# Loading the weights' 64-row remainders first, on two queues, and alternating two V products in the first step

## The chip, the cores and the metric

The kernel runs on one core of a Trainium2 chip. The metric is the device time of one execution in microseconds. TensorE (PE) does the matrix products, VectorE (DVE) and ScalarE (ACT) the elementwise work and the copies out of PSUM, GpSimd (POOL) some fills and a power, and SyncE (SP) issues most transfers. ACT and POOL can issue transfers too, each on a queue of its own.

## The reference

Two layers of the same kind run one after the other over 2048 rows of width 576. Each layer adds a memory-augmented attention, and then a gated feed-forward block:

```
for s in range(n_seg):                      # 64 segments of 32 rows
    h = concat([mem, x[s]])                 # 8 memory rows + 32 rows, width 576
    q, k, v = h @ Wq, h @ Wk, h @ Wv        # 32 heads of 128
    p = softmax(where(mask, q @ k.T * scale, -1e9))
    o = (p @ v) @ Wo
    mem = o[:8]; out[s] = o[8:]
x = x + attention(layernorm(x));  x = x + (silu(n @ w1) * (n @ w3)) @ w2   # n = layernorm(x)
```

The memory makes the 64 segments of a layer a chain: a segment's first products need the memory rows that the segment before it gave.

## The kernel before

The kernel works in steps. Step t does segment t of the first layer and, eight steps later, the segment of the second layer that has become ready, so there are 72 steps and the first eight hold one layer only. The width of 576 is four blocks of 128 rows and a remainder of 64 rows; every product with Wq, Wk and Wv has a part for the four blocks and a part for the remainder.

The weights stay in SBUF. Tile W (128 x 9 x 4096) holds the four blocks of Wq in places 0 to 3 and those of Wk in places 4 to 7; place 8 holds the remainder of Wq in partitions 0 to 63 and that of Wk in partitions 64 to 127. Tile WV holds the four blocks of Wv and then its remainder, the even groups of 512 columns in partitions 0 to 63 and the odd ones in 64 to 127. Wo goes to WO in four groups of eight heads. All of it is loaded once, at the start, on SP's queue, in this order: load_qk for the first half of the heads (eight pieces of 512 KB, then two remainder pieces of 256 KB), load_qk for the second half, load_v (four blocks of 1 MB, then two remainder pieces of 256 KB), load_o (four groups). ACT's queue brings the first 128 rows of x (tile XN) and the first memory (load_m0).

A step's products are these. QK units 0 to 7 (four heads each) make q and k, in qk (32 matmuls in step 0) and qk_tail (8). A score (SC), a softmax, a transposition of the probabilities (TR), the product of probabilities and V (PV) and the product with Wo (WO and its tail) follow for each of four groups of heads. V is made in v_mm, for two sets of rows: vx for the rows of x (VX) and vm for the strip with the memory rows (VM). In step 0 each has 32 main matmuls, four blocks of Wv by two banks by four column strips, and 8 for the remainder. Each of the two sets fills two PSUM banks, and eight evictions of 512 columns by ACT or DVE (v_ev) bring them into tile V.

Everything is laid down by a planner (plan). make_nodes writes the program as nodes with an engine, a modelled duration, what they depend on, a priority and the buffers that they take and free. The planner then simulates: for each engine it takes the node that could start first, and among several the one with the lowest priority number. A node of engine "AD" goes to ACT or to DVE, whichever can take it. The modelled order on each engine is kept in the program. PE alone isn't chosen in this way: its order is written out by hand as a string of letters (FIRST for the beginning), a letter for each node: Q and q for a QK unit's blocks and remainder, S for scores, T for TR, P for PV, O and o for WO, X and x for VX's main part and remainder, V and v for those of VM. In v_nodes the evictions depend on both parts; those of VX have priority -0.77 in step 0, those of VM 0.14.

Records of engine instructions stand on the lines of the helpers: L578 matmuls, L581 ACT, L584 DVE, L587 transfers on SP's queue, L590 on ACT's, L593 on POOL's.

Of the kernel before, what the change touches and what calls it, by code (L numbers as in the profile page):

```python
# [9 lines left out]
ACT = mybir.ActivationFunctionType  # L10
# [3 lines left out]
P = 128  # L14
R64 = 64
D = 576
# [10 lines left out]
NG = 4  # L27
# [157 lines left out]
def ewh(*ns):  # L185
# [2 lines left out]


FIRST = (  # L190
    "maQqqqQQSQqqqQTQSqqQSQSXxvVPTPTOPOTOoooPOoQQQqqVSqqvQQqqSQQqqSQTXPSxTOPTPOTOPoooOoaQQqqqqQSvQVSqQQqTQSqqQSPTPOOT"
    "ooPTPOOooQQqqqvqSVQQQqSTQqqQPSqQOSoTXPTOPTOPxooOoQQpQqqqqQSVSnvqQFffqFQQTSqqPQOToSfFPWTOPfFTOPFOfoooWQQfqqqQSvVF"
    "qfQFQWSqqQFSfQTQPqqfFOTSoWPFTOPfxXTFPOOoooWQQqqfqQQSfqFSvVfqqQFQWSqTQQPFqffTOSoPWOTFPFTOPfaOoooWQFQqqfQSVvqqfFQQ"
    "SqWQQqqqQSTPSTbOPoXTOPTxxPOOoooXqqQpQQqqSVvnQFFSfqQqfqQQTSqfFPQTOPSofWTOPFOTFPWOoooFQqqffQQqSQQQqqgqGTSWPQQfqqFF"
# [21 lines left out]
class Opt:  # L216

    qk, qkt, sc, tr, pv, wo, wog, vm = 0.0079, -0.0342, 0.0268, 0.1447, 0.0406, 0.2653, 0.0725, 0.1407
    vmt, vx, vxt, ff, fft, win, w2, gstep = -0.0231, 0.2313, 0.0843, 0.2124, -0.1839, 0.8 * (LAG - 4), 0.1943, 0.0624
    ustep, mode_pen, hor, wait, bulk, ff_split, last_win, tail_at = 0.0315, 0.1194, 0.0162, 0.141, 0.02, False, 2.5, -1.5  # L220


def make_nodes(em, nseg, pools, o=Opt, dma_bw=230e3, load_bw=400e3):
# [4 lines left out]
    def node(*a, **k):  # L228
        n = Node(*a, **k)
        nodes.append(n)  # L230
        return n

    def banks(n=2):
        return [Slot("bank") for _ in range(n)]

    nst = nseg + LAG
    kb = lambda rows, cols: rows * cols * 2
# [9 lines left out]
    def load(name, nbytes, prio, fn, deps=()):  # L247
        return node("DMA", nbytes / load_bw, fn, deps=deps, prio=prio, name=name, lat=2.0)

    ld_m0 = node("ACT", 0.1, em.load_m0(), prio=-90, name="m0", lat=2.5)  # L250
    ld_h = [load("ldqk", kb(512 + 2 * R64, 4096), half - 9.0, em.load_qk(half)) for half in (0, 1)]
    ld_v = [load("ldv", kb(512 + 2 * R64, 4096), -7.0, em.load_v())]
    ld_o = [load("ldo", kb(1024, 576), g - 6.0, em.load_o(g)) for g in range(NG)]

    b = banks(1)
# [303 lines left out]
class Emitter:  # L559
# [79 lines left out]
    def load_qk(self, half):  # L639
        def f(n):  # L640
            h = slice(half * 2048, (half + 1) * 2048)
            for kind, wd in ((0, self.a.wq), (1, self.a.wk)):
                for c in range(4):
                    self.dma(self.T.W[:, 4 * kind + c, h], wd[c * P:(c + 1) * P, h])
            for kind, wd in ((0, self.a.wq), (1, self.a.wk)):
                self.dma(self.T.W[kind * R64:(kind + 1) * R64, 8, h], wd[4 * P:D, h])
        return f

    def wv(self, tail):
# [4 lines left out]
    def load_v(self):  # L654
        def f(n):
            for c in range(4):
                self.dma(self.wv(False)[:, c, :], self.a.wv[c * P:(c + 1) * P, :])
            for r in (0, 1):
                self.dma(self.wv(True)[r * R64:(r + 1) * R64, :].rearrange("p (q n) -> p q n", q=NG),
                         self.a.wv[4 * P:D, :].rearrange("p (q r n) -> r p q n", q=NG, r=2)[r])  # L660
        return f

    def load_o(self, g):
# [131 lines left out]
        return lambda n: self.cp(n, self.T.XTB[:, :, bi * P:(bi + 1) * P], self.lnps(b))  # L795


    def v_mm(self, t, b, strips, tail):

        HTt = self.ht(t)  # L800
        W = self.wv(tail)
        first = self.begin(b)
        for c in ((4,) if tail else range(4)):
            for r in (0, 1):
                for p0, c0, q, m, row in strips:
                    out = self.bk(b[r])[p0:p0 + m, :]
                    if tail:
                        rr = slice(r * R64, (r + 1) * R64)
                        self.mm(out, HTt[rr, 4, c0:c0 + m], W[rr, q * 512:(q + 1) * 512], first, True, tile_position=(r * R64, p0))
                    else:  # L810
                        w0 = (2 * q + r) * 512
                        self.mm(out, HTt[:, c, c0:c0 + m], W[:, c, w0:w0 + 512], first and c == 0, c == 3, tile_position=(0, p0))

    def vg(self, t, g, b, tail):

# [33 lines left out]
        return [(p0, m, row, 2 * q + r) for p0, _, q, m, row in strips]  # L849

    def vx(self, t, k, b, tail):
        return lambda n: self.v_mm(t, b, self.vx_strips(t, k), tail)

    def vm(self, t, k, b, tail):
        return lambda n: self.v_mm(t, b, self.vm_strips(t, k), tail)

    def v_ev(self, b, p0, width, row, blk):
        return lambda n: self.cp(n, self.T.V[row:row + width, blk, :], self.bk(b)[p0:p0 + width, :])
# [317 lines left out]
def kernel(  # L1176
# [26 lines left out]
    em = Emitter(nc, tc, T, a, nseg)  # L1203
    pools = dict(POOLS)
    nodes = make_nodes(em, nseg, pools)

    wp = ctx.enter_context(tc.tile_pool(name="wts", bufs=1))
# [94 lines left out]
```

## Time and profile before

| | us |
|---|---|
| median of 4 runs | 2703.91 |
| lowest and highest | 2702.74, 2704.65 |
| the profiled execution, its own time | 2701.56 |
| its span in the profile | 2699.8 |
| PE busy | 2628.1 (97%) |
| DVE busy | 2090.4 (77%) |
| ACT busy | 1367.3 (51%) |
| mean granted PE clock | 0.993 |

The profile is one execution. Its time lies 1.76 us above its span, and 2.35 us below the median of the four runs. Times of instructions are counted from the start of the span. Brackets behind an instruction give the engine's idle time before it and what ended it. "PEclk" is the granted share of PE's clock. The DMA share is the mean busy share of 16 DMA engines.

### The profile page before, as it was taken

The numbers are of one execution on the slowest core, as the hardware profiler recorded it, in microseconds if no ns is written. First come the engines' busy times: TensorE is split into PE (matmuls) and PEld (weight loads), VectorE is DVE, ScalarE is ACT, GpSimd is POOL, SyncE is SP. The second block draws the span as 40 slices with busy tenths as digits, with TensorE's granted clock in tenths as the row PEclk, the third lists the DMA queues.
The fourth block names the chain that finished last, engine by engine and source line by source line (L and its number), as shares of the span: only waits on it lengthen the run. The fifth ranks groups of instructions, "written<-read, shape, count | busy, mean of one in ns | idle before, by whom it ended". The sixth has DMA issues, their size and how long they took to land.

```text
span 2699.8 us, 126553 instructions
## 1 busy us (share of the span) xinstructions
PE 2628.1 (97%) x55714; PEld 2225.9 (82%) x55795; DVE 2090.4 (77%) x5376; ACT 1367.3 (51%) x4025; POOL 333.6 (12%) x400
## 2 busy tenths in 40 slices
PE   5999999999999999999999999999999999999998
PEld 3788888888888888888888888888888888888886
DVE  4777887877778777777877777787787777787876
ACT  2655554545545454554545455464544546454553
POOL 1111110110101011010101101010110101011110
PEclk8999999999999999999999999999999999999999
DMA  9064524234342423434243343433334342434358
GB/s 316 4 186 123 159 84 118 80 110 126 99 134 80 121 86 110 125 102 131 79 119 88 110 125 96 129 87 115 92 110 125 96 129 70 128 95 141 114 157 262
DMA packets 483225, 321.42 MB, mean 119 GB/s; under 512 B 26376, under 2 KB 477328, under 8 KB 482160
## 3 DMA queue, kind: packets, MB, share of 16 engines
q1 hardware_dynamic: 479488, 306.22, 38.5%
q8 instruction: 437, 7.16, 1.1%
q0 software_dynamic: 3024, 6.93, 0.9%
q14 instruction: 116, 0.95, 0.1%
q10 hardware_dynamic: 160, 0.16, 0.0%
HBM read 308.49 MB, written 2.36 MB: 115 GB/s over the span
## 4 chain that ended last, share of the span: by engine, by line
PE 87%; ACT 4%; DVE 3%; DMA 3%; issue 1%; SPq 1%; POOL 0%; DVEq 0%; ACTq 0%; POOLq 0%
PE bank L578 87%; ACT V L581 3%; DMA W<-in_B_w_dram 2%; DVE SME L584 1%; DMA W<-in_A_Wk_dram 1%; DVE STAT L584 1%; DMA WV<-in_A_Wv_dram 1%; DVE V L584 1%; SPq L587 1%; ACT SME L581 0%; ACT XTB L581 0%; ACT PTS L581 0%; ACT QKT L581 0%; DVE PB L584 0%; DVE OT L584 0%
## 5 line engine op out<-in xcount | busy, mean ns | idle before, releaser
L578 PEld LDWEIGHTS <-W 128*128 128x128 bf16 (+1 forms) x29520 | 1237.8, 98 | 148.2 <-issue 43.6
L578 PE MATMUL bank<-HT,W 128*128 128x80 bf16 (+3 forms) x23040 | 811.2, 196 | 22.7 <-DMA W<-in_A_Wq_dram 10.3
L578 PE MATMUL bank<-XTB,W 128*128 128x256 bf16 (+3 forms) x6480 | 661.0, 261 | 7.1 <-DMA W<-in_B_w_dram 6.1
L581 ACT ACTIVATE QKT<-bank 128x256 bf16<-128x256 f32 (+3 forms) x1587 | 365.9, 316 | 368.8 <-PE bank L578 349.9
L981 POOL MEMSET PB<- 128x1024 bf16 x288 | 274.2, 952 | 1815.9 <-PE bank L578 1303.4
L578 PE MATMUL bank<-OT,WO 128*128 128x80 bf16 (+3 forms) x11520 | 406.0, 198 | 0.6 <-DVE OT L584 0.3
L581 ACT ACTIVATE V<-bank 64x512 bf16<-64x512 f32 (+1 forms) x616 | 346.5, 584 | 109.4 <-PE bank L578 104.2
L578 PEld LDWEIGHTS <-WO 128*128 128x128 bf16 (+1 forms) x11520 | 378.7, 102 | 15.6 <-issue 5.6
L578 PE MATMUL bank<-WV,HT 128*32 128x512 bf16 (+5 forms) x3160 | 357.1, 385 | 14.8 <-issue 8.8
L578 PE MATMUL bank<-W2C,HTT 128*128 128x288 bf16 x2240 | 315.1, 286 | 0.0
L584 DVE TENSOR_TENSOR PB<-SME,STAT 40x128 bf16<-40x128 f32 (+4 forms) x912 | 275.3, 336 | 14.9
L584 DVE TENSOR_REDUCE STAT<-SME 104x8 f32<-104x320 f32 (+1 forms) x576 | 273.9, 476 | 13.6 <-ACT SME L581 8.3
L581 ACT ACTIVATE HTT<-bank 128x512 bf16<-128x512 f32 (+1 forms) x324 | 179.6, 555 | 181.9 <-PE bank L578 179.9
L578 PEld LDWEIGHTS <-HT 128*32 128x32 bf16 (+4 forms) x3240 | 137.1, 97 | 158.0 <-issue 39.7
L584 DVE SCALAR_TENSOR_TENSOR XR<-bank,XR 128x288 f32<-128x288 f32 x576 | 246.8, 450 | 16.6 <-PE bank L578 8.5
L578 PEld LDWEIGHTS <-HTT 128*128 128x128 bf16 x2304 | 210.4, 98 | 48.7 <-issue 0.2
L581 ACT ACTIVATE OT<-bank 128x320 bf16<-128x320 f32 (+1 forms) x398 | 149.3, 405 | 167.1 <-PE bank L578 165.9
L584 DVE CAST QKT<-bank 128x192 bf16<-128x192 f32 (+2 forms) x461 | 125.0, 317 | 136.2 <-PE bank L578 134.8
L584 DVE SCALAR_TENSOR_TENSOR HTT<-HTT,bank 128x512 bf16<-128x512 bf16 (+1 forms) x324 | 202.5, 625 | 33.8 <-ACT HTT L581 30.0
L584 DVE TENSOR_TENSOR HTT<-HTT,bank 128x512 bf16<-128x512 bf16 (+1 forms) x324 | 203.7, 629 | 30.6 <-DVE HTT L584 0.5
L581 ACT ACTIVATE PTS<-bank 128x320 bf16<-128x320 f32 (+1 forms) x385 | 144.4, 401 | 162.7 <-PE bank L578 123.6
L581 ACT ACTIVATE SME<-SME 104x320 f32<-104x320 f32 (+1 forms) x288 | 135.5, 470 | 139.7 <-DVE SME L584 136.9
(61 smaller groups left out, 1804.9 us busy)
## 6 DMA issues: line engine op xcount, KB each, us to landing
W<-in_B_w_dram SPq DMA_DIRECT2D x612, 256.0 KB, 3.5
W2C<-in_B_w_dram SPq DMA_DIRECT2D x306, 288.0 KB, 3.2
W<-in_B_w_dram SPq DMA_DIRECT2D x612, 32.0 KB, 3.3
W<-in_B_w_dram SPq DMA_DIRECT2D x16, 512.0 KB, 8.7
WO<-in_A_Wo_dram SPq DMA_DIRECT2D x4, 1152.0 KB, 16.3
XR<-in_A_x_dram POOLq DMA_DIRECT2D x16, 288.0 KB, 2.8
WV<-in_B_w_dram SPq DMA_DIRECT2D x8, 576.0 KB, 7.3
W<-in_A_Wq_dram SPq DMA_DIRECT2D x8, 512.0 KB, 8.9
```

The source lines that it names most:

```text
L578: self.ch("PE", self.nc.tensor.matmul(out, lhsT=lhsT, rhs=rhs, start=start, stop=stop, skip_group_check=True, **k))
L581: self.ch("ACT", self.nc.scalar.activation(*a, **k))
L584: self.ch("DVE", getattr(self.nc.vector, fn_)(*a, **k))
L587: self.ch("SP", self.nc.sync.dma_start(out=out, in_=in_))
L981: return lambda n: self.ch("POOL", self.nc.gpsimd.memset(self.T.PB[:, pb.i], 0.0))
```

## The change

Three things change.

The remainders are no longer loaded with their halves. A new load_tails brings them first: SP's queue gets the whole remainder of Wq (64 rows of 4096 columns, partitions 0 to 63) and the lower half of Wv's; ACT's queue gets the whole remainder of Wk (partitions 64 to 127) ahead of x, and the upper half of Wv's behind the first memory.

In step 0 vx no longer emits its main matmuls. It keeps its banks and rows, and vm emits them together with its own: for each block of Wv first those of VX, then those of VM.

In FIRST the letters "XxvV" of step 0 become "XVxv".

```
 FIRST = (
-    "maQqqqQQSQqqqQTQSqqQSQSXxvVPTPTOPOTOoooPOo...
+    "maQqqqQQSQqqqQTQSqqQSQSXVxvPTPTOPOTOoooPOo...
...
-    ld_h = [load("ldqk", kb(512 + 2 * R64, 4096), half - 9.0, em.load_qk(half)) for half in (0, 1)]
-    ld_v = [load("ldv", kb(512 + 2 * R64, 4096), -7.0, em.load_v())]
+    ld_t = [load("ldt", kb(3 * R64, 4096), -10.0, em.load_tails(0)), node("ACT", 0.1, em.load_tails(1), prio=-120, name="ldt", lat=6.0)]
+    node("ACT", 0.1, em.load_tails(2), prio=-80, name="ldt", lat=6.0)
+    ld_h = [load("ldqk", kb(512, 4096), half - 9.0, em.load_qk(half)) for half in (0, 1)]
+    ld_v = [load("ldv", kb(512, 4096), -7.0, em.load_v())]
...
-            for kind, wd in ((0, self.a.wq), (1, self.a.wk)):
-                self.dma(self.T.W[kind * R64:(kind + 1) * R64, 8, h], wd[4 * P:D, h])
+    def load_tails(self, what):
+        def f(n):
+            if what < 2:
+                d, wd = (self.dma, self.a.wq) if what == 0 else (self.adma, self.a.wk)
+                d(self.T.W[what * R64:(what + 1) * R64, 8, :], wd[4 * P:D, :])
+            if what != 1:
+                r = what // 2
+                (self.adma if r else self.dma)(self.wv(True)[r * R64:(r + 1) * R64, :].rearrange("p (q n) -> p q n", q=NG),
+                                               self.a.wv[4 * P:D, :].rearrange("p (q r n) -> r p q n", q=NG, r=2)[r])
+        return f
...
-            for r in (0, 1):
-                self.dma(self.wv(True)[r * R64:(r + 1) * R64, :].rearrange("p (q n) -> p q n", q=NG),
-                         self.a.wv[4 * P:D, :].rearrange("p (q r n) -> r p q n", q=NG, r=2)[r])
...
-    def v_mm(self, t, b, strips, tail):
+    def v_mm(self, t, sets, tail):
...
-        first = self.begin(b)
+        sets = [(b, strips, self.begin(b)) for b, strips in sets]
         for c in ((4,) if tail else range(4)):
-            for r in (0, 1):
-                for p0, c0, q, m, row in strips:
+            for b, strips, first in sets:
+                for r in (0, 1):
+                    for p0, c0, q, m, row in strips:
...
     def vx(self, t, k, b, tail):
-        return lambda n: self.v_mm(t, b, self.vx_strips(t, k), tail)
+        def f(n):
+            if t == 0 and not tail:
+                self.x0 = (b, self.vx_strips(t, k))
+                return
+            self.v_mm(t, [(b, self.vx_strips(t, k))], tail)
+        return f
...
-        return lambda n: self.v_mm(t, b, self.vm_strips(t, k), tail)
+        return lambda n: self.v_mm(t, ([self.x0] if t == 0 and not tail else []) + [(b, self.vm_strips(t, k))], tail)
```

More of the change, by code (lines that the diff above doesn't have):

```diff
@@ L190 @@
 FIRST = (
-    "maQqqqQQSQqqqQTQSqqQSQSXxvVPTPTOPOTOoooPOoQQQqqVSqqvQQqqSQQqqSQTXPSxTOPTPOTOPoooOoaQQqqqqQSvQVSqQQqTQSqqQSPTPOOT"
+    "maQqqqQQSQqqqQTQSqqQSQSXVxvPTPTOPOTOoooPOoQQQqqVSqqvQQqqSQQqqSQTXPSxTOPTPOTOPoooOoaQQqqqqQSvQVSqQQqTQSqqQSPTPOOT"
     "ooPTPOOooQQqqqvqSVQQQqSTQqqQPSqQOSoTXPTOPTOPxooOoQQpQqqqqQSVSnvqQFffqFQQTSqqPQOToSfFPWTOPfFTOPFOfoooWQQfqqqQSvVF"
@@ L795, in xtb_write @@
         return lambda n: self.cp(n, self.T.XTB[:, :, bi * P:(bi + 1) * P], self.lnps(b))
-    def v_mm(self, t, b, strips, tail):
+    def v_mm(self, t, sets, tail):
         HTt = self.ht(t)
         W = self.wv(tail)
-        first = self.begin(b)
+        sets = [(b, strips, self.begin(b)) for b, strips in sets]
         for c in ((4,) if tail else range(4)):
-            for r in (0, 1):
-                for p0, c0, q, m, row in strips:
[L806 to L812, printed above, removed]
+            for b, strips, first in sets:
+                for r in (0, 1):
+                    for p0, c0, q, m, row in strips:
+                        out = self.bk(b[r])[p0:p0 + m, :]
+                        if tail:
+                            rr = slice(r * R64, (r + 1) * R64)
+                            self.mm(out, HTt[rr, 4, c0:c0 + m], W[rr, q * 512:(q + 1) * 512], first, True, tile_position=(r * R64, p0))
+                        else:
+                            w0 = (2 * q + r) * 512
+                            self.mm(out, HTt[:, c, c0:c0 + m], W[:, c, w0:w0 + 512], first and c == 0, c == 3, tile_position=(0, p0))
     def vg(self, t, g, b, tail):
```

## The prediction

> **What bounds the kernel now.** I read the shares of busy time first: PE is busy 97% of a span of 2699.8 us, and only the first of the 40 slices shows it half idle. The change touches nothing but the first load of the weights and the V products of step 0, so the question is how much earlier step 0 can end, since all later work hangs on it. The windows view of that stretch (columns: length, then busy us and count of PE, PEld, DVE, ACT, POOL, then PEclk, DMA share, GB/s):
>
> ```profile
> 14.00:17.00 3.00, 2.58 (x39) 1.39 (x37) 0.00 (x0) 0.00 (x0) 0.00 (x0) 1.00 1.03 229
> 18.00:26.00 8.00, 3.16 (x117) 2.95 (x112) 3.53 (x10) 1.71 (x6) 0.00 (x0) 0.94 1.03 408
> 27.00:30.00 3.00, 0.00 (x0) 0.00 (x0) 0.00 (x0) 0.00 (x0) 0.00 (x0) 0.50 1.06 238
> 32.00:39.00 7.00, 5.89 (x184) 5.49 (x184) 4.10 (x12) 1.65 (x6) 0.95 (x1) 0.77 1.01 419
> 40.00:46.00 6.00, 2.32 (x36) 0.81 (x29) 2.87 (x9) 0.68 (x2) 0.00 (x0) 0.96 1.08 222
> 46.00:55.00 9.00, 6.83 (x100) 3.29 (x99) 6.59 (x12) 5.99 (x14) 1.44 (x2) 0.50 1.08 389
> ```
>
> The DMA engines are busy throughout, yet move half as much in three stretches. Those are just the stretches of the 64-row remainders: of Wq and Wk for the first half of the heads, for the second half, and of Wv. Now PE's timeline, for what waits on them:
>
> ```profile
> 31.46 0.21 PE L578 MATMUL bank<-HT,W 64*128 64x40 bf16 x1 [10.30 <-DMA W<-in_A_Wq_dram]
> 32.36 1.63 PE L578 MATMUL bank<-HT,W 64*128 64x40 bf16 x47 [0.68 <-DMA W<-in_A_Wk_dram]
> ...
> 39.75 1.48 PE L578 MATMUL bank<-WV,HT 128*32 128x512 bf16 x24
> 43.94 0.62 PE L578 MATMUL bank<-WV,HT 128*32 128x512 bf16 x8 [2.71 <-DMA WV<-in_A_Wv_dram]
> 45.27 0.47 PE L578 MATMUL bank<-WV,HT 64*32 64x512 bf16 x4 [0.72 <-DMA WV<-in_A_Wv_dram]
> 46.36 4.58 PE L578 MATMUL bank<-WV,HT 64*32 64x512 bf16 x44 [0.61 <-DMA WV<-in_A_Wv_dram]
> 51.20 0.31 PE L578 MATMUL bank<-PTS,V 128*128 128x40 bf16 x4 [0.26 <-ACT V L581]
> ...
> 59.53 1.19 PE L578 MATMUL bank<-OT,WO 128*128 128x40 bf16 x40 [0.27 <-ACT OT L581]
> ```
>
> The reader is to see: x's V product does three blocks of Wv (24 matmuls), waits 2.71 us for the fourth, then for each half of the remainder. Only then do the strip's 32 main matmuls begin, inside the 44. PE's clock is 0.50 by then, and the first P.V product comes at 51.20, released by an eviction of V. ACT's timeline shows those evictions, four of x and four of the strip:
>
> ```profile
> 45.79 2.39 ACT L581 ACTIVATE V<-bank 32x512 bf16<-32x512 f32 x4 [3.02 <-PE bank L578]
> 50.56 2.51 ACT L581 ACTIVATE V<-bank 32x512 bf16<-32x512 f32 x4 [2.38 <-PE bank L578]
> ```
>
> [...] 4 KB packets take about 159 ns when 128 rows are written, about 286 ns in the remainders. [...] at 4 to 5 us x (ACT's queue) and Wq (SP's) move together at 389 GB/s. Two half-partition transfers at once appear nowhere in this trace. [...] here the clock is 0.50 from 25 to 35 and from 45.5 to 59 us[...].
>
> **The load, step by step.** Sizes are from the DMA issues: four 256 KB pieces of Wq and Wk remainders (1.05 MB), two of Wv (0.52 MB), 1.57 MB in all. Removed ahead of Wv's last block are two pairs of 0.52 MB at 229 and 238 GB/s: 2.3 + 2.2 = 4.5 us. Added at the front are all six (now four issues of 512, 512, 256 and 256 KB). At the full 408 GB/s they take 3.85 us; at 229, 6.9 us. The price of pairing is unknown: the 16 engines could all be on the lower half together and then on the upper, which would gain nothing. I take 370 GB/s, near the top[...]: 4.25 us. So the mains of the first half come 4.25 us later, those of the second half 2 us later than now, Wv's blocks 0.25 us earlier.
>
> The semaphore events of the trace give each transfer's 16 shares: Wv's fourth block arrives from 39.81 to 43.90. Its late shares fall into the slow stretch of the remainders behind it; a Wo piece, with nothing slow behind it, spreads over 2.3 us (46.78 to 49.09). New arrival of the whole block: 39.81 - 0.25 + 2.3 = **41.9** instead of 43.9; 41.5 with perfect pairing, 44.5 with none.
>
> **What comes late at the front, and its cover.** Wk's remainder goes ahead of x and mem0 on ACT's queue; the fourth issue follows them. ACT itself first computes at 11.58, so some 0.5 us per issue cost nothing. SP's queue gets two issues more at its head and six fewer later. x landed 5.47; with 1.05 MB ahead it lands at 8 to 10. The layer norm on DVE waited for DVE's own memsets until 8.36 anyway, so HT is written up to 1.7 us later than 13.84, while the first QK needs Wk's fourth block, now at 15.5 + 4.25 = 19.7. Cover 4 us. POOL issues nothing of this.
>
> QK units 0 to 3 (15.97 to 21.16 now) end at about 25.1, and the remainder products of units 3 to 5 follow at once: 24 matmuls, some 0.7 us. Then PE waits for the second half's mains, at about 30.5 instead of 32.35 for its last remainder. The 7.4 us from there to the V products shrink by 15 remainder matmuls (0.4 us): V starts at about 37.5. Its 48 matmuls for three blocks, at 1.48/24 = 0.062 each, end at 40.5, inside the wait for 41.9. Alternation so puts 24 strip matmuls where PE idled; were the clock half, they'd end at about 43.4 and cost 1.5 us of the gain.
>
> **From Wv's last block to P.V.** Left are 16 main matmuls, at 0.060 each (32 in 1.91 us in the next step, full clock): 0.96 us; then x's remainder, 8 in 0.41, whose first half frees the first bank after 0.2: the first eviction starts 1.2 us after the block. The strip's remainder lies beside it. But x and strip now finish together, so no matmuls of the strip hide x's evictions: eight of x must pass ACT and DVE (0.588 and 0.686 each) before the strip's first, by the priorities. Five on ACT are 3.0 us. So P.V comes 4.2 us after the block, 46.1, where it took 7.3. **Gain 5.1 us.** The 3.1 us less than now are: 24 strip matmuls and two remainder waits gone, partly paid back by naked evictions. Half clock would cost 0.96 + 0.2 more, gain 3.9.
>
> From there to the end of the step ACT, DVE and PE have the same work in the same order as from 51.20 on, at the same half clock[...]. I let the shift pass unchanged. One bound: Wo's last group. The view by tile says:
>
> ```profile
> L587 SPq DMA_DIRECT2D WO<-in_A_Wo_dram x4: 385/4479/7723, 31.4 to 46.2; - x4
> ...
> DMA to landing us min/median/max: 12.5/16.3/19.8
> ```
>
> The last is issued at 46.2 and lands 12.5 later, 58.7, for products at 59.53. Its stretch gets back 2.0 us (the W remainders at full rate) and 2.6 (1.33 MB in 40 to 46 us, against 3.4 us at 389 GB/s): 54.1. Shifted by 5.1 the products start at 54.4. So it just holds, and caps the gain near 5.4 to 6.
>
> **Sum.** Against the profiled execution: 2701.56 - 5.1 = 2696.5 (span 2699.8 to 2694.7). That execution lies 2.35 under the median of four, 2703.91, so against the median: 2698.8; I say 2698.9. About 0.2%, 5.4 us, is what a measurement can tell from no change, so the forecast lies just inside it.
>
> **Rivals.**
> Pairing does nothing (the change doesn't do what it says): the remainders take 6.9 us at 229 GB/s, the block lands at 44.5, P.V at 48.7, gain 2.5: 2701.4. [...]
>
> The load gains more: engines stay closer together, so shares spread over 1 us and not 2.3, Wo's last group comes as much earlier, and the clock stays full through the O products (groups of 32 in 0.96 instead of 1.23 us, some 1.5 us in all). Gain 6 to 8: 2696.9. For it: the early Wq blocks spread over 0.8 us only. Against: Wv's first, unslowed by remainders, already spread over 2.2.
>
> Slower: the orders of ACT and DVE for the whole program come from a planner's modelled times; only PE's order is written out. The new nodes shift those times. If later evictions thereby fall behind another on their engine, each 0.30 us QKT eviction so delayed in all of the 72 steps costs 21.6 us: 2703.9 - 5 + 21.6 = 2720.5. It decides from 0.15 us per step (5 + 5.4 over 72). For it: ACT and DVE share evictions by the model. Against: past step 0 PE sets the model's times as well, so a pure shift leaves the choices as they were.
>
> **How the numbers follow.** The forecast, 0.72, with its own range of 3.6 to 6.2 us gain (half clock to perfect pairing and shorter spread): 0.30 of it beyond 5.4 us, 0.42 within. Pairing void 0.10, within. More gain 0.10, faster. Slower 0.08. Sums: 0.40 faster, 0.52 the same, 0.08 slower. Range 2696.0 to 2703.0: it holds the forecast, the void pairing and most of the larger gain, and leaves out the planner's case and the ends.
>
> **What would show it.** Right: over 350 GB/s from 2 to 7 us and no dip at 14, 27 and 40; V's matmuls in runs of 16; Wv's last block at about 42; P.V at about 46; Wo's last group near 54. Wrong: a first 1.5 MB at 230 GB/s, a clock of 0.5 through the V products, evictions of the strip ahead of x's, or a distance from P.V to the end that isn't what it was.

## The result, and the profile after

| | before | after |
|---|---|---|
| median of all runs, us | 2702.74 (62 runs) | 2698.44 (43 runs) |
| ratio to before, 95% interval | | 0.9985, 0.9981 to 0.9989 |
| span of the profiled execution, us | 2699.8 | 2695.9 |

The ratio makes the gain 4.1 us (0.0015 of 2702.7), with an interval from 3.0 to 5.1 us. That is less than 0.2%, as forecast; the forecast gain was 5.0 us. The forecast had the gain's size. It did not have the way to it.

First the windows view of the kernel after, over the stretches that were shown of the kernel before; the columns are the same, and the last number is GB/s:

```profile
14.00:17.00 3.00, 0.00 (x0) 0.00 (x0) 0.00 (x0) 1.21 (x5) 0.00 (x0) 1.00 1.02 406
18.00:26.00 8.00, 7.92 (x173) 5.26 (x173) 1.73 (x5) 0.91 (x3) 0.00 (x0) 1.00 1.03 410
27.00:30.00 3.00, 0.19 (x1) 0.10 (x1) 1.23 (x4) 0.20 (x1) 0.00 (x0) 1.00 1.02 407
32.00:39.00 7.00, 5.36 (x148) 5.01 (x149) 4.22 (x12) 1.47 (x5) 0.95 (x1) 0.59 1.02 420
40.00:46.00 6.00, 4.45 (x87) 1.98 (x86) 4.66 (x12) 2.46 (x5) 0.00 (x0) 1.00 1.06 382
```

The three slow stretches at 14, 27 and 40 us are gone. They have moved to the front, as these windows of the same profile show:

```profile
2.50:6.50 4.00, 0.00 (x0) 0.00 (x0) 3.67 (x6) 0.00 (x0) 3.34 (x10) 1.00 1.02 233
9.00:13.00 4.00, 1.00 (x10) 0.76 (x11) 2.38 (x10) 0.03 (x1) 0.56 (x1) 1.00 1.04 335
```

233 GB/s is the half rate of the kernel before (229 and 238). The DMA packets of the trace say how: the 64 packets of 8 KB of SP's queue (Wq's remainder) begin between 2.10 and 4.02 us, the 64 of ACT's queue (Wk's) between 3.97 and 6.40. There were two queues and both issues began at 0.75 us, and the halves were still written one after the other.

PE's timeline of the kernel after, through step 0 (matmuls are now recorded on line L580):

```profile
31.40 0.21 PE L580 MATMUL bank<-HT,W 128*128 128x40 bf16 x1 [1.09 <-DMA W<-in_A_Wk_dram]
32.67 1.01 PE L580 MATMUL bank<-HT,W 128*128 128x40 bf16 x25 [1.06 <-DMA W<-in_A_Wk_dram]
...
40.28 4.19 PE L580 MATMUL bank<-WV,HT 128*32 128x512 bf16 x80
47.35 0.27 PE L580 MATMUL bank<-PTS,V 128*128 128x40 bf16 x4 [2.88 <-ACT V L583]
...
55.52 1.19 PE L580 MATMUL bank<-OT,WO 128*128 128x40 bf16 x40 [0.29 <-ACT OT L583]
```

The second half of Wk releases PE at 32.67, where its remainder did at 32.36: the load has gained nothing there. The V products start half a microsecond later than before. But then all 80 run in one piece, with no wait for Wv, and the P.V products come 3.85 us earlier than 51.20. Ahead of them stands the bare wait for V's evictions, 2.88 us. They make one run on ACT:

```profile
44.30 4.79 ACT L583 ACTIVATE V<-bank 32x512 bf16<-32x512 f32 x8 [1.00 <-PE bank L580]
```

The last WO products start 4.0 us earlier than 59.53, and the span is 3.9 us shorter: in this pair of profiles what step 0 gained reached the end. That the two agree so well is chance. The same kernel profiled again (e11) started the last WO products at 58.04, only 1.5 us earlier than before, and its span was 2.6 us shorter (2697.2). From the start of the second step to the end, the fourteen profiles of this document took between 2636.1 and 2644.5 us.

### The profile page after: what moved, and what is told of

Same layout as the page of the kernel before. It is cut to its first block, busy times and chain, and to the rows that moved or that the text cites. A ratio compares the mean times of both kernels' runs of the same rounds, so it can differ in the third digit from the quotient of the medians.

```text
span 2695.9 us, 126547 instructions
## 1 busy us (share of the span) xinstructions
PE 2624.4 (97%) x55714; PEld 2224.5 (83%) x55795; DVE 2089.9 (78%) x5376; ACT 1366.6 (51%) x4025; POOL 333.2 (12%) x400
## 4 chain that ended last, share of the span: by engine, by line
PE 87%; ACT 4%; DVE 3%; DMA 3%; issue 1%; SPq 0%; POOL 0%; ACTq 0%; DVEq 0%; POOLq 0%
PE bank L580 87%; ACT V L583 3%; DMA W<-in_B_w_dram 2%; DVE SME L586 1%; DMA W<-in_A_Wk_dram 1%; DVE STAT L586 1%; DVE V L586 1%; SPq L589 0%; ACT SME L583 0%; DMA WV<-in_A_Wv_dram 0%; ACT XTB L583 0%; ACT QKT L583 0%; ACT PTS L583 0%; DVE PB L586 0%; DVE OT L586 0%
## 5 line engine op out<-in xcount | busy, mean ns | idle before, releaser
L580 PEld LDWEIGHTS <-W 128*128 128x128 bf16 (+1 forms) x29520 | 1238.0, 98 | 143.2 <-issue 44.8
L580 PE MATMUL bank<-HT,W 128*128 128x80 bf16 (+3 forms) x23040 | 812.1, 197 | 18.2 <-ACT HT L583 6.3
L580 PE MATMUL bank<-XTB,W 128*128 128x256 bf16 (+3 forms) x6480 | 660.9, 261 | 6.2 <-DMA W<-in_B_w_dram 5.1
L580 PE MATMUL bank<-OT,WO 128*128 128x80 bf16 (+3 forms) x11520 | 406.1, 198 | 0.8 <-DVE OT L586 0.5
L580 PEld LDWEIGHTS <-WO 128*128 128x128 bf16 (+1 forms) x11520 | 378.8, 102 | 15.8 <-issue 5.8
L580 PE MATMUL bank<-WV,HT 128*32 128x512 bf16 (+5 forms) x3160 | 353.6, 381 | 12.0 <-issue 10.0
L580 PE MATMUL bank<-W2C,HTT 128*128 128x288 bf16 x2240 | 315.2, 286 | 0.0
L580 PEld LDWEIGHTS <-HT 128*32 128x32 bf16 (+4 forms) x3240 | 136.5, 96 | 152.8 <-issue 33.2
L580 PEld LDWEIGHTS <-HTT 128*128 128x128 bf16 x2304 | 209.7, 98 | 48.6 <-issue 0.4
```

The source lines that it names most:

```text
L580: self.ch("PE", self.nc.tensor.matmul(out, lhsT=lhsT, rhs=rhs, start=start, stop=stop, skip_group_check=True, **k))
```

## Experiments

All ratios are to the kernel before, with the 95% interval. Where two kernels are compared, each was run beside the kernel before on the same chip; medians of different groups of runs aren't compared, since the kernel before's own median lies between 2700.72 and 2702.74 us from group to group. Theory A, formed on the traces: the second queue does nothing, the remainders cost at the front what they cost elsewhere, and the gain is that nothing slow stands behind a block that PE waits for. Theory B: two queues save load time. Theory C, the prediction's: the alternation brings most of the gain.

### Each part alone

e1_load_only has the new load and the old V order; e10_load_only_again is the same kernel once more; e11_changed_again is the changed kernel beside it.

```
-    "maQqqqQQSQqqqQTQSqqQSQSXVxvVPTP...
+    "maQqqqQQSQqqqQTQSqqQSQSXxvVPTP...
-            if t == 0 and not tail:
+            if False:
-        return lambda n: self.v_mm(t, ([self.x0] if t == 0 and not tail else []) + [(b, ...
+        return lambda n: self.v_mm(t, [(b, self.vm_strips(t, k))], tail)
```

> The new order of the load alone; step 0's V products in the old order (x's four blocks, x's remainder, the strip's remainder, the strip's four blocks). Theory A (the new load order alone brings the gain: nothing slow stands behind Wv's last block any more, so all of Wv is there by 42.6 us, and the alternation only trades hidden evictions against hidden products): x's products end near 43.6 us, their eight evictions run beside the strip's 32 products at full clock (2 us), P.V starts at 46.5 to 47.0 instead of 47.35, ratio to the kernel before 0.998 to 0.9985, gain 4 to 5 us. Rival C (the alternation brings the gain, as the prediction had it: 3.1 of its 5.1 us): P.V at 49 to 50.5 us, gain under 2 us.

> The new order of the load alone, a second time, beside the changed kernel on the same chip. If the alternation is worth nothing once the load is in the new order: within 1 us of the changed kernel's median. If the alternation is worth the 24 products that it takes out of the end of the V products, at half clock 2.5 us, less the evictions it lays bare: the changed kernel 1 to 2 us faster than this.

> The changed kernel itself, beside the new load order alone. Ratio to the kernel before 0.998 to 0.999 as on record; its difference to the load order alone is the alternation's worth: 0 if the alternation is worth nothing once the load is in the new order, 1 to 2 us otherwise.

e2_alternate_only keeps load_qk, load_v and make_nodes' load lines of the kernel before, and takes the rest of the change.

> The alternating V products of step 0 alone; the old order of the load. Theory A: Wv's last block comes at 43.9 us and its remainder's two halves at 45.3 and 46.3 as in the kernel before, so evictions can't start before about 46.2 us; five on ACT later P.V starts at 49.3 to 49.8 us instead of 51.2, gain 1.5 to 2 us. Rival C: P.V at 47 to 48 us, gain 3 to 4 us. If neither part reaches the whole change's 4 us alone, they need each other.

| | ratio | interval |
|---|---|---|
| new load alone, first time | 0.9990 | 0.9982 to 0.9998 |
| new load alone, second time | 0.9988 | 0.9981 to 0.9995 |
| changed kernel, first time | 0.9985 | 0.9981 to 0.9989 |
| changed kernel, beside the second | 0.9991 | 0.9983 to 0.9999 |
| alternation alone | 1.0004 | 0.9996 to 1.0012 |

The new load alone gains 2.7 and 3.2 us, less than the 4 to 5 that its theory asked for but with the changed kernel's value inside both intervals. Beside each other, load alone and the changed kernel can't be told apart: by the means of these runs the changed kernel is 1.2 us the slower, give or take 1.5. The alternation alone gains nothing that can be seen, against both expectations. PE's timeline, first of e1_load_only (two lines), then of e2_alternate_only:

```profile
40.27 5.97 PE L580 MATMUL bank<-WV,HT 128*32 128x512 bf16 x80
47.29 0.27 PE L580 MATMUL bank<-PTS,V 128*128 128x40 bf16 x4 [1.04 <-ACT V L583]
```

```profile
40.53 2.77 PE L578 MATMUL bank<-WV,HT 128*32 128x512 bf16 x48
44.72 1.05 PE L578 MATMUL bank<-WV,HT 128*32 128x512 bf16 x16 [1.42 <-DMA WV<-in_A_Wv_dram]
46.33 0.40 PE L578 MATMUL bank<-WV,HT 64*32 64x512 bf16 x4 [0.56 <-DMA WV<-in_A_Wv_dram]
47.53 0.61 PE L578 MATMUL bank<-WV,HT 64*32 64x512 bf16 x12 [0.80 <-DMA WV<-in_A_Wv_dram]
49.83 0.32 PE L578 MATMUL bank<-PTS,V 128*128 128x40 bf16 x4 [1.69 <-ACT V L581]
51.52 0.31 PE L578 MATMUL bank<-PTS,V 128*128 128x40 bf16 x4 [1.38 <-DVE V L584]
...
59.43 1.21 PE L578 MATMUL bank<-OT,WO 128*128 128x40 bf16 x40 [0.47 <-DMA WO<-in_A_Wo_dram]
```

In the first, x's evictions run beside the strip's products, so only 1.04 us of eviction is left to wait for; the changed kernel pays 2.88. The V products themselves took 5.97 us and not 4.19, and P.V came at the same time all the same. As 4.19 us is their length at a clock of 1.00, 5.97 makes a mean clock of about 0.70, an estimate: half clock for a part of them. In the second, the runs of 48 and 16 show that the alternation does fill the wait for the last block, as predicted, but the two halves of the remainder come at 46.33 and 47.53, and the evictions follow bare: 1.69 and 1.38 us. The second half of the first P.V products starts at 51.52, where the kernel before had 51.73. At the end of the step the last WO products then wait for Wo's last group, which comes in the old load's time, and start at 59.43 instead of 59.53. So the old load leaves the alternation nothing to gain, and with the new one no run shows a gain from it. Theory C falls.

### One queue or two

e5_one_queue is the changed kernel with the four transfers on SP's queue:

```
+            for r, wd in ((0, self.a.wq), (1, self.a.wk)):
+                self.dma(self.T.W[r * R64:(r + 1) * R64, 8, :], wd[4 * P:D, :])
+            for r in (0, 1):
+                self.dma(self.wv(True)[r * R64:(r + 1) * R64, :]...
```

> The changed kernel with all four remainder transfers on SP's queue one after another (x and the first memory alone on ACT's). Theory A (in the changed kernel the halves ran one after the other in spite of two queues, at about 205 GB/s): the same rate at the front, Wk's last block of the second half within 0.7 us of 32.6, and the time within 1 us of the changed kernel's. Rival B (two queues do save load time): everything up to the V products 2 us later or more, gain on the kernel before 2 us or less.

Ratio 0.9987 (0.9980 to 0.9993). The windows view of this kernel:

```profile
2.50:6.50 4.00, 0.29 (x5) 0.20 (x5) 3.67 (x6) 0.00 (x0) 3.35 (x10) 1.00 1.03 236
```

236 GB/s on one queue, 233 on two. PE got Wk's last block at 31.96 us, 0.7 earlier than with two queues. Theory B falls.

### Finer turns between the queues

e4_slices cuts Wq's and Wk's remainders into four transfers each, still one tensor to a queue. It ran once, for its profile, so it has no ratio:

```
-                d(self.T.W[what * R64:(what + 1) * R64, 8, :], wd[4 * P:D, :])
+                for i in range(4):
+                    d(self.T.W[what * R64:(what + 1) * R64, 8, i * 1024:(i + 1) * 1024], wd[4 * P:D, i * 1024:(i + 1) * 1024])
```

> The changed kernel with the remainders of Wq and Wk each in four transfers of 1024 columns instead of one of 4096, Wq's on SP's queue and Wk's on ACT's as before. Theory D [...]: the slices of the two queues now take turns, packets of both queues show within the same microsecond,[...] the rate at the front stays at 200 to 250 GB/s and P.V within 1.5 us of the changed kernel's. Theory E (once both queues are served at the same time the halves add up): over 300 GB/s from 2.5 to 5.5 us, and Wk's last block of the second half 1.5 us earlier.

```profile
2.50:6.50 4.00, 0.00 (x0) 0.00 (x0) 3.67 (x6) 0.00 (x0) 3.34 (x10) 1.00 0.90 253
```

Now 2 KB packets of both queues appear within each microsecond from 3 us on (57 and 74, 72 and 69), so here the two queues run side by side. The rate is 253 GB/s in this window, with 289 in its best microsecond: a little above what theory D allows (200 to 250), below theory E (over 300). Wk's last block of the second half came at 32.54, 0.13 us earlier. Running side by side did not bring the 408 GB/s of the blocks. Whether the engines were all on one half at a time, as the prediction feared, the trace doesn't show, as it has no engine for a packet. P.V came 2.5 us later than in the changed kernel's profile, but by the V products' clock (6.48 us for 80, about 0.65 by the estimate from 4.19 us at 1.00), not by the load.

### What perfect pairing would be worth

e7_full_partitions writes the same bytes to all 128 partitions:

```
+                c = slice(what * 2048, (what + 1) * 2048)
+                d(self.T.W[:, 8, c], wd[4 * P - R64:D, c])
```

(and Wv's alike).

> The changed kernel with the same number of bytes in each of the four remainder transfers, but written to all 128 partitions with half the columns (128 rows of Wq, Wk and Wv from row 448 on): the remainder weights are wrong by that, all other data and all instructions are the changed kernel's. It prices what a perfect pairing of the halves would have been worth. The prediction's perfect pairing: 1.57 MB in 3.85 us at 408 GB/s where the changed kernel took some 7 us, Wk's last block of the second half 2.5 to 3 us earlier (30 us), P.V at 44.5 to 45.5 us, gain on the kernel before 6 to 7.5 us, ratio 0.9973 to 0.9978. If it is the QK units and evictions that bound step 0 and not the load: within 1 us of the changed kernel.

Ratio 0.9976 (0.9969 to 0.9983), a gain of 6.5 us. The windows view and PE's timeline of this kernel:

```profile
2.50:6.50 4.00, 0.00 (x0) 0.00 (x0) 3.67 (x6) 0.00 (x0) 3.34 (x10) 1.00 0.96 331
```

```profile
29.51 1.01 PE L580 MATMUL bank<-HT,W 128*128 128x40 bf16 x25 [1.06 <-DMA W<-in_A_Wk_dram]
...
37.26 5.54 PE L580 MATMUL bank<-WV,HT 128*32 128x512 bf16 x80
45.68 0.27 PE L580 MATMUL bank<-PTS,V 128*128 128x40 bf16 x4 [2.88 <-ACT V L583]
```

The whole chain up to the V products moves by 3.0 to 3.2 us against the changed kernel. So the first load still bounds step 0, and the half rate costs about 2.4 us of the kernel's time (6.5 - 4.1, give or take 2.2 by the two intervals). This kernel leaves the remainders' weights wrong; it is a price, not a version.

### Where the slow transfers may stand

e6_wv_rest_late moves Wv's remainder from the front to right ahead of Wv's first block, on SP's queue.

```
+            for r in (0, 1):
+                self.dma(self.wv(True)[r * R64:(r + 1) * R64, :]...
             for c in range(4):
                 self.dma(self.wv(False)[:, c, :], self.a.wv[c * P:(c + 1) * P, :])
```

> The changed kernel with the two transfers of Wv's remainder on SP's queue right ahead of Wv's first block, and no more at the front. The QK units of the second half then find their last block 2 to 2.5 us earlier (30.1 to 30.7 us, not 32.7), V's products start at 37.5 to 38.5 us, and have to wait for Wv's last block again, at 42.5 to 43.5 us. If the load bounds step 0 as a whole: V's products end at 44 to 45 us and the time is within 1 us of the changed kernel's, ratio to the kernel before 0.998 to 0.9987. If the QK units' wait for the second half bounds it, as the changed kernel's profile reads: P.V 2 us earlier than in the changed kernel, ratio 0.9978.

```profile
27.72 0.21 PE L579 MATMUL bank<-HT,W 128*128 128x40 bf16 x1 [2.54 <-DMA W<-in_A_Wk_dram]
29.30 0.21 PE L579 MATMUL bank<-HT,W 128*128 128x40 bf16 x1 [1.36 <-DMA W<-in_A_Wk_dram]
32.06 1.02 PE L579 MATMUL bank<-HT,W 128*128 128x40 bf16 x25 [2.54 <-DMA W<-in_A_Wk_dram]
```

Ratio 0.9987 (0.9979 to 0.9995). PE's timeline shows Wk's third block of the second half early, at 29.30, and the fourth only at 32.06, 2.76 us behind it, where the changed kernel has 1.27. The block did not wait behind the remainder: the remainder stands behind it. A transfer gives 16 semaphore events, its shares, read here as one for each DMA engine. Of the third block the last share came at 29.26, 1.8 us after the other 15. Of the fourth, 15 were there by 29.07, while the last came at 32.02, 3.0 us behind them: a few 4 KB packets of the block are still seen between 29 and 31 us, among those of the slow remainder. PE went on at 32.06, 0.04 us after the last share. Of the expected 2 to 2.5 us, 0.6 were left (32.06 for 32.67), and the V products started at 39.77. The kernel before had slow remainders behind such a block three times.

### Evictions by group

e3_group_evictions gives x's evictions of step 0 the strip's priority; e8_late_and_group adds that to e6.

```
-                ... prio=prio + 0.01 * (blk // 2),
+                ... prio=(prio if t else o.vm) + 0.01 * (blk // 2),
```

> The changed kernel, with x's evictions of V in step 0 at the strip's priority, so that the planner takes them group by group: P.V of group 0 needs 4 evictions and not 10. If bare evictions are what P.V waits for (2.88 us in the changed kernel): P.V of group 0 at 45.5 to 46.0 us instead of 47.35. The end of the step moves less, since Wo's last group comes at 54.7 us for products that now start at 55.5: at most 0.8 us gained on the changed kernel, a wait for Wo appearing at the last WO products. Rival: the other groups' evictions only come later by as much, and the WO products of the last group start at 55.5 as before, no gain at all.

> Wv's remainder right ahead of Wv's blocks and x's evictions of V in step 0 at the strip's priority, on top of the changed kernel: both edits that free an end of the same stretch. If each hides behind the other when alone, together they gain 1 to 2 us on the changed kernel, P.V of group 0 at 45.5 to 46.5 us, ratio to the kernel before 0.998 or less; if Wo's last group, at 54.7 us, is the bound, the last WO products wait for it and the gain on the changed kernel stays under 0.8 us.

e3: ratio 0.9985 (0.9979 to 0.9992). Its V products took 5.88 us, a mean clock of about 0.71 by the same estimate, so P.V came at 47.24 and not at 45.5. The wait ahead of P.V fell from 2.88 to 1.07 us, and the later groups gave some of it back: waits of 0.61 and 0.41 us appear among the WO and TR products, and the last WO products start at 55.65. In the time no gain on the changed kernel can be seen, as its rival had it; the two profiles differ in PE's clock, so they don't settle what the order of the evictions is worth. e8: ratio 0.9996 (0.9987 to 1.0004), no gain that can be seen. PE's timeline of e8 has the announced wait:

```profile
55.95 1.37 PE L579 MATMUL bank<-OT,WO 128*128 128x40 bf16 x40 [1.28 <-DMA WO<-in_A_Wo_dram]
```

So Wo's last group is the next bound, as the prediction had it. Why e8 is no better than that, when its profiled execution was 3.1 us shorter than the one of before (2696.7), stays open.

### Another queue, and the simplest version

e9_pool_queue issues the four remainders on POOL's queue (swdma), beside the blocks on SP's.

> The changed kernel with the four remainder transfers on POOL's queue, behind POOL's first fills (issued from about 6 us on[...]), so that they run beside the blocks of Wq and Wk on SP's queue. If a lower-half and an upper-half transfer on this queue are written at the same time[...]: over 370 GB/s throughout from 7 to 17 us, Wk's last block of the second half at 30 us, gain as with full partitions, ratio 0.9973 to 0.9982. If the halves run one after another here too: two dips to 250 to 350 GB/s, Wk's last block of the second half within 1 us of the changed kernel's 32.7, ratio 0.9982 to 0.999; if the slow packets delay the block beside them, or POOL's issue time holds up the layer norm's power, worse than that, 0.999 to 1.0005.

Ratio 0.9995 (0.9987 to 1.0003): the worst of its cases. The windows view of e9:

```profile
7.00:17.00 10.00, 2.15 (x8) 0.96 (x9) 3.56 (x13) 2.24 (x5) 2.02 (x4) 1.00 1.01 292
17.00:27.00 10.00, 6.26 (x102) 3.42 (x102) 0.32 (x1) 0.34 (x2) 0.00 (x0) 1.00 1.03 342
```

The slow packets now run in the midst of the blocks, hold both at 205 to 274 GB/s from 11 to 21 us, and Wk's last block of the second half comes at 34.02. POOL's four issues took from 6.00 to 8.45 us and ended before its power at 9.70; they did no harm.

e12_first_one_queue is e5's load with the old V order: the remainders first, on SP's queue, and nothing else.

> The simplest part: the four remainder transfers first, all on SP's queue, and nothing else of the change (x alone ahead on ACT's queue, V products in the old order). If what gains is only that no remainder stands behind a block any more: Wk's last block of the second half at 32.0 us, P.V at 46.0 to 47.0 us, ratio to the kernel before 0.9983 to 0.999, the same as the changed kernel's. If two queues or the alternation are needed for the gain: ratio over 0.9992.

Ratio 0.9984 (0.9975 to 0.9993), a gain of 4.3 us: the changed kernel's, with neither the second queue nor the alternation. PE's timeline of e12:

```profile
32.27 1.01 PE L579 MATMUL bank<-HT,W 128*128 128x40 bf16 x25 [1.05 <-DMA W<-in_A_Wk_dram]
...
40.02 6.08 PE L579 MATMUL bank<-WV,HT 128*32 128x512 bf16 x80
46.95 0.27 PE L579 MATMUL bank<-PTS,V 128*128 128x40 bf16 x4 [0.84 <-ACT V L582]
```

e5 differs from it in the V products' order alone. PE's timeline of e5:

```profile
39.75 5.88 PE L579 MATMUL bank<-WV,HT 128*32 128x512 bf16 x80
48.51 0.27 PE L579 MATMUL bank<-PTS,V 128*128 128x40 bf16 x4 [2.88 <-ACT V L582]
```

With V products about as long in both (6.08 and 5.88 us, a mean clock of about 0.69 and 0.71 by the same estimate), the alternating order has P.V 1.6 us later, as it leaves the evictions bare. In the time (0.9987 against 0.9984) the two can't be told apart. e12 bears out theory A: of the change, it is the place of the remainders that gains.

## Why the prediction was right, and where its steps were not

**Pairing, the first step, failed.** By pairing the prediction means that a transfer to the lower 64 partitions and one to the upper 64, on two queues, are written at once and together come near the full rate. The 370 GB/s taken for it, "near the top", was the author's estimate; 233 were measured. Two things were wrong in it. The large transfers of the two queues, Wq's and Wk's, did not run at the same time, and where they did, in e4, the rate was still only 253. The first half's last block came 6.9 us later by its first share (20.74 instead of 13.88), just the bound for no pairing, and not 4.25; by its last share it came 5.6 us later (21.10 instead of 15.49), as no slow remainder stood behind it any more. For the second half the forecast was 30.5 and the measured time 32.67. The rival "Pairing does nothing" happened, yet its price was wrong as well: it had a gain of 2.5 us.

**The arrival of Wv's last block was put too late.** For the void pairing the prediction had 44.5; the semaphore events of the trace after have its shares from 40.89 to 42.59. Two terms were mis-sized. The slow stretches had cost the blocks that followed them more than their own length: Wv's first block came 2.48 us behind Wk's last, by their first shares, where it had been 5.41 with 2.2 to 2.3 us of remainders between; that is 0.6 us, and 0.5 more lay between the two halves. And the spread of the shares was 1.7 us, not 2.3. The reading that Wv's first block "unslowed by remainders, already spread over 2.2" was wrong in part: it stood right behind remainders. In the kernel after, 15 of its shares come within 0.4 us, and the last 1.3 us behind them, so 1.7 us remain.

That late share goes with something that the prediction did not look for. From 14 to 26 us all 16 shares of a block of W come within 0.4 us. At 26.31 us the trace has one packet of 16 KB of the kind "instruction", 1.08 us long, and from the block whose first share is at 27.14 us on, one share of each is late. After the second such packet, at 36.20, two are late, and after the third, at 42.47, three. The trace gives no engine for a packet; that one engine carries it and stays behind is the author's reading of these counts, and isn't shown. PE's wait at 32.67 was ended by such a share (32.63, the other 15 by 31.30).

**The QK units took 7.6 us to the V products, not 7.0.** PE was at half clock for most of it (0.59 over 32 to 39 us). With the late start this put V at 40.28 instead of 37.5. In the kernel before, the half clock from 45.5 to 59 us came after pauses of 2.71 and 0.72 us among the V products; what sets the clock no run here shows.

**The 3.1 us between Wv's last block and P.V were not the alternation's.** That stretch did become shorter in the profile, by 2.5 us (from 7.30 to 4.76). The sum had it from "24 strip matmuls and two remainder waits gone", less the bare evictions, all against the kernel before. But e1, with the load alone, has P.V at 47.29 as well: the waits go by the new load, and in the old order the strip's matmuls hide x's evictions. Once Wv is there in time, no gain is left of it (0.9988 without and 0.9991 with it, side by side), and with V products of about 6 us the bared evictions cost more than the moved matmuls save (P.V at 48.51 in e5, 46.95 in e12).

**From Wv to P.V** the terms held where the clock did: five evictions on ACT took 3.05 us from 44.30 to 47.35, for a predicted 3.0. P.V at 46.1 was measured at 47.35. The full clock was luck: of the twelve profiles with the new load or a variant of it, eleven have V products of 5.3 to 6.6 us (the longest, 6.58 in e11, at a measured mean clock of 0.63), and only this one has 4.19, at 1.00.

**The rest held in this profile.** The shift passed to the end (3.85 us at P.V, 4.0 at the last WO products, 3.9 in the span). Wo's last group, the cap, was issued at 42.75 and landed 11.9 us later, at 54.7, against 54.1. That too is luck in part: 2.0 us of the sum were to come from W's remainders at full rate, which they didn't reach; instead its first share came 2.9 us earlier and its shares closer together (1.8 for 2.9 us). x and the layer norm were late as said (PE's transposes of x at 12.18 instead of 10.79) and well ahead of PE's next work, at 17.30.

**The planner's rival** can be read from the programs: the orders of ACT, DVE, POOL and SP differ from those before in the moved transfers and in one pair of evictions of step 0, an OT and a PTS that change engines. All later steps are the same.

So the total came out near the forecast because a load 2.6 us dearer than taken (6.9 against 4.25) was offset by blocks that arrive in better order, and not because each step was right. That the two came out even was luck.

## What to carry to other kernels

A transfer that ran at half rate delayed not only what was behind it but also the block right ahead of it: in e6 the last share of that block came 3.0 us behind the other 15, and PE went on only then. So put such transfers where nobody waits for their neighbours, first of all if PE has nothing to do there anyway. Before two halves are put on two queues to fill each other's gaps, run the same two on one queue: here it was the same (236 GB/s on one, 233 on two). And when a change has two parts, price the second in the state that the first leaves behind, not in the state of the old kernel.

## What the runs showed of the hardware that was not expected

- Two transfers of 512 KB to 64 partitions each, on two queues and both issued at 0.75 us, ran one after the other: 233 GB/s from 2.5 to 6.5 us, where the blocks from 14 to 30 us have 406 to 410. The prediction took them to run at once. Each is 64 packets of 8 KB in the trace, and the second queue's first packet begins at 3.97 us, the first queue's last one at 4.02. Packets of two queues within one microsecond are seen in the kernel before (4 KB of Wq and 1152 bytes of x, 2 to 5 us) and in e4 (2 KB slices). What decides when packets of the second queue begin no run here shows.
- One packet of 16 KB of the kind "instruction", some 1.08 us long, goes with one more late share in every block behind it: none before the first, then one, two and three. So it is in the profiles of the changed kernel (26.31, 36.20 and 42.47 us), e1 (26.28, 36.13 and 42.49), e10 and e11; the late shares come 1.2 to 1.4 us behind the others. No run tries to move these packets.
- PE's clock decided a good part of one execution's time. The 80 V products took 4.19 us at a clock of 1.00 in one profile of the changed kernel and 6.58 us at 0.63 in another, with P.V at 47.35 and 49.97. The windows view of the two:

```profile
40.28:44.47 4.19, 4.19 (x83) 1.76 (x80) 3.16 (x10) 0.68 (x3) 0.00 (x0) 1.00 1.04 374
```

```profile
40.52:47.10 6.58, 6.58 (x83) 2.31 (x80) 3.17 (x10) 0.65 (x2) 0.00 (x0) 0.63 1.07 381
```

- Later in the program single windows of 3.41 us at half clock come and go from run to run (226.37 to 229.78 us in the kernel before, 99.18 to 102.59 in the changed one). Within the span, e1's profile has 18.7 us of half clock after the first 70 us, and the changed kernel's 6.8; e1 began its second step 4.3 us ahead of the kernel before and yet had a span 1.5 us longer (2701.3). Runs of one kernel lie up to 13 us apart (before: 2698.12 to 2711.19), so a profile tells where a microsecond went in step 0, and only many runs tell what it is worth.
